# One decode layer on one core: a single ordered stream of cache loads over six 32 KB tiles, with the projections and the ending in column layout

## The chip, the cores and the metric

The kernel runs on one core of a Trainium2 chip. The metric is device time in microseconds (us). Quoted times are medians of the executions in the fast state; the spans in the profiles are about 2 us shorter than the device time. A ratio is the mean time of one kernel's fast runs over the mean of the kernel before's fast runs of the same rounds, so it is not quite the ratio of the medians.

How to read the profile: PE is TensorE's products, PEld its weight loads, DVE is VectorE, ACT ScalarE, POOL GpSimd, SP SyncE; "SPq" is SP's instruction queue. "L147" is line 147 of the kernel that the profile belongs to. A bracket such as `[1.36 <-issue]` gives the idle time of the engine before the instruction and what ended it; "issue" means that the engine waited for nothing that the profile shows.

## The reference, cut to what matters

```python
B, Sq, D, H, Sk, Dh, F = 2, 1, 512, 32, 8192, 128, 1376      # all data bf16
n = layernorm(x)                                            # [B, 1, D]
q = (n @ wq).reshape(B, 1, H, Dh)                           # wq [512, 4096]
p = softmax(q . k_cache * Dh**-0.5)                         # k_cache [B, H, 8192, 128]
o = p @ v_cache                                             # v_cache [B, H, 8192, 128]
h = x + o.reshape(B, 1, H * Dh) @ wo                        # wo [4096, 512]
g = layernorm(h)
out = h + (relu(g @ W_gate) * (g @ W_up)) @ W_down           # F = 1376
```

One token of each of two sequences attends to 8192 cached keys and values, each head with its own cache. K and V are 134 MB each, and every byte is used once. All the weights together are 12.6 MB.

## The kernel before

It takes the 64 heads of both batch entries one after the other. K of a head is a 16 KB row in each of 128 partitions, and VectorE makes the scores of one head: a product with q (the same in all partitions), four halving additions and a reduction. TensorE makes p·V for two heads at a time, with p as the two-column stationary operand and V moving. The parts that the change touches:

```python
# q: 64 products with one output row; the row goes through DRAM to be spread over the partitions
with tc.tile_pool(name="wq", bufs=1) as wq_pool, tc.tile_pool(name="qc", bufs=3) as qcpool:
    wq_sb = wq_pool.tile([P, KC, Hq * Dh], bf16)                 # 32 KB a partition
    nc.sync.dma_start(out=wq_sb, in_=...)
    for b in range(B):
        for n8 in range(NQC):
            # ... 4 matmuls into qps [1, 512], copied to qch [1, 512] ...
            nc.sync.dma_start(out=qdram[b, n8 * 512:(n8 + 1) * 512], in_=qch[0:1, :])
# the wq pool ends here, and the pools below get its space
qrep = qrep_pool.tile([P, B, Hq * Dh], bf16)
nc.sync.dma_start(out=qrep, in_=qdram_b)                         # partition step 0: 2.1 MB
kpool (3 x 16 KB), vgpool (2 x 32 KB), prodpool (2 x 16 KB) = ...

for b in range(B):
    for g in range(NG):                                          # two heads
        for j in range(G):                                       # one head
            nc.sync.dma_start(out=kt, in_=A_k_cache[b, h]...)    # K on SP's queue
            nc.scalar.dma_start(out=vg[:, j], in_=A_v_cache[b, h]...)   # V on ACT's
            nc.vector.tensor_tensor(out=prod, in0=kt, in1=qh, op=ALU.mult)
            # ... halving adds in prod, reduce to scol, exp into pg, the sum of p ...
        for t in range(NT):
            nc.tensor.matmul(out=ops[2, 256], lhsT=pg[:, :, t], rhs=V of both heads at t, ...)

# attention's pools end here; only then is there room for wo
nc.gpsimd.dma_start(out=wo_sb, in_=A_wo.rearrange("(h d) n -> d h n", d=P))
# ... W_gate, W_up, W_down on the SP and ACT queues ...
for b in range(B):
    for h in range(Hq):                                          # rows of 512
        nc.tensor.matmul(out=aps[1, 512], lhsT=ocols[:, b, h:h + 1], rhs=wo_sb[:, h, :], ...)
    # residual and layernorm on one partition
# ... gate and up: weights stationary, 2 columns moving; down: rows of 512 again ...
```

The softmax here doesn't subtract the row's maximum and nothing guards it: scores larger than these inputs give would overflow.

## Time and profile before

| | before |
|---|---|
| median of 4 runs beside the changed kernel (lowest to highest) | 721.05 us (720.52 to 723.4) |
| span in the profile | 719.8 us |
| DMA: bytes, mean rate | 283.56 MB, 394 GB/s |
| VectorE busy | 602.4 us, 84% |
| TensorE products busy, mean granted clock | 346.4 us, 0.744 |

The kernel is bound by its loads. These lines of its profile page show VectorE's busy share in tenths, the DMA engines' busy share in tenths, and the rate, in 40 equal slices of 18.0 us:

```profile
...
DVE  1007999999999999999999989999999999999612
...
DMA  9739699999999999999999999999999999999970
GB/s 371 328 154 429 249 420 383 429 426 428 427 427 425 429 423 427 430 426 427 428 425 428 427 427 427 425 427 427 428 425 429 426 425 428 428 424 432 343 267 1
...
```

VectorE starts late and is then nearly as busy as DMA. From 126 us to 665 us every slice moves about 427 GB/s. At that rate 283.56 MB take 664 us. The rest of the 719.8 us is lost in holes, and they can be added up from the last row: in the first seven slices (371, 328, 154, 429, 249, 420, 383) some 27.6 us, in the last four (432, 343, 267, 1) some 28.0 us, and in between next to nothing. The Trainium skill ("DMA: Bandwidth & Descriptors", Where 436 GB/s comes from) gives the fabric's ceiling as 435 GB/s; 427 is 2% under it.

The largest early hole, in a table of stretches (after the busy times and counts of PE, PEld, DVE, ACT and POOL come PE's granted clock, the DMA engines' busy share and the GB/s):

```profile
...
30.00:40.00 10.00, 10.00 (x43) 3.64 (x42) 0.00 (x0) 5.89 (x11) 0.00 (x0) 1.00 0.20 83
40.00:46.00 6.00, 4.26 (x20) 1.52 (x19) 0.00 (x0) 4.54 (x7) 0.00 (x0) 1.00 0.00 1
46.00:50.00 4.00, 0.00 (x0) 0.00 (x0) 0.00 (x0) 0.23 (x1) 0.00 (x0) 0.89 0.74 262
...
```

From 30 to 46 us, while TensorE makes q, less than 1 MB is loaded. The costliest groups of instructions (after the bar: busy time, mean ns of one; after the second bar: idle time just before them, and what ended most of it):

```profile
...
L170 DVE TENSOR_TENSOR prod<-kt,qrep 128x8192 bf16<-128x8192 bf16 x64 | 283.2, 4425 | 72.9 <-DMA kt<-in_A_k_cache_dram 72.9
...
L250 PE MATMUL aps<-wo_sb,ocols 128*1 128x512 bf16 x64 | 14.0, 379 | 1.1 <-DMA wo_sb<-in_A_wo_dram 1.1
...
L309 PE MATMUL dps<-wd_sb,hmlp_cols 128*1 128x512 bf16 (+1 forms) x22 | 7.8, 540 | 0.5 <-DVE hmlp_cols L296 0.5
...
```

VectorE waits for K for 72.9 us in all. In the ending, 64 wo products of 512 columns take 14.0 us, and the 22 of W_down 7.8 us. The same ending holds the cheap form as well. In the timeline (start, duration, instruction, count), gate and up have weights stationary and only two columns moving, and four products start every 0.11 us, one per 27 ns:

```profile
...
705.38 0.25 PE L278 MATMUL gu_ps<-hncols,wg_sb 128*128 128x2 bf16 x4 [0.26 <-ACT hncols L271]
...
705.49 0.25 PE L285 MATMUL gu_ps<-hncols,wu_sb 128*128 128x2 bf16 x4
...
```

### The profile page before, as it was taken

The page shows a single profiled execution, that of the slowest core. Times are in us where ns is not written, and L with a number is a line of the kernel's source. Part 1 is how long each engine was busy: PE and PEld are TensorE (multiplying, and loading weights), DVE is VectorE, ACT ScalarE, POOL GpSimd, SP SyncE. Part 2 cuts the span into 40 slices and gives each one's busy share as a digit, 9 for nine tenths or more (in the row PEclk, how much of TensorE's full clock was granted, in tenths as well). Part 3 has the DMA queues.
Part 4 walks back from the last instruction along what each step waited for, and adds up shares of the span by engine and source line. Part 5 has one row for each costly group of instructions (what it writes and reads, how often), then busy time and mean ns, then how long its engine had stood idle before and what let it go on. Part 6 is the DMA issues. An engine that isn't in the chain of part 4 may idle for free.

```text
span 719.8 us, 6035 instructions
## 1 busy us (share of the span) xinstructions
PE 346.4 (48%) x2431; PEld 221.6 (31%) x2431; DVE 602.4 (84%) x412; ACT 60.2 (8%) x252; POOL 3.7 (1%) x12
## 2 busy tenths in 40 slices
PE   0440454554443455455544444554555444444896
PEld 0110233332232333333332223333333322333543
DVE  1007999999999999999999989999999999999612
ACT  1140000000000000000000000000000000000010
POOL 1000000000000000000000000000000000000000
PEclk9985577787667776777777776677776777667797
DMA  9739699999999999999999999999999999999970
GB/s 371 328 154 429 249 420 383 429 426 428 427 427 425 429 423 427 430 426 427 428 425 428 427 427 427 425 427 427 428 425 429 426 425 428 428 424 432 343 267 1
DMA packets 22735, 283.56 MB, mean 394 GB/s; under 512 B 2242, under 2 KB 3636, under 8 KB 5684
## 3 DMA queue, kind: packets, MB, share of 16 engines
q1 hardware_dynamic: 11748, 143.25, 47.6%
q10 hardware_dynamic: 9856, 135.73, 44.7%
q0 software_dynamic: 1104, 4.20, 1.7%
q8 instruction: 19, 0.31, 0.2%
q14 instruction: 8, 0.07, 0.0%
HBM read 283.15 MB, written 0.02 MB: 393 GB/s over the span
## 4 chain that ended last, share of the span: by engine, by line
DMA 47%; DVE 40%; issue 7%; PE 6%; ACT 0%; SPq 0%; DVEq 0%; POOLq 0%; ACTq 0%
DMA kt<-in_A_k_cache_dram 41%; DVE prod L170 21%; DVE prod L174 18%; DMA wq_sb<-in_A_wq_dram 4%; DMA wo_sb<-in_A_wo_dram 2%; PE qps L121 2%; PE aps L250 2%; PE dps L309 1%; DVE scol L182 1%; PE gu_ps L278 0%; PE gu_ps L285 0%; DMA qdram<-qch 0%; DVE stats L78 0%; DVE h_rows L256 0%; DVE outr L316 0%
## 5 line engine op out<-in xcount | busy, mean ns | idle before, releaser
L201 PE MATMUL ops<-vg,pg 128*2 128x256 bf16 x2048 | 294.1, 316 | 252.8 <-DMA vg<-in_A_v_cache_dram 220.5
L170 DVE TENSOR_TENSOR prod<-kt,qrep 128x8192 bf16<-128x8192 bf16 x64 | 283.2, 4425 | 72.9 <-DMA kt<-in_A_k_cache_dram 72.9
L201 PEld LDWEIGHTS <-pg 128*2 128x2 bf16 x2048 | 196.6, 97 | 392.0 <-issue 232.1
L174 DVE TENSOR_TENSOR prod<-prod 128x4096 bf16<-128x4096 bf16 (+3 forms) x256 | 281.7, 1155 | 0.0
L186 ACT ACTIVATE pg<-scol 128x64 bf16<-128x64 f32 x64 | 16.4, 256 | 366.9 <-DVE scol L182 366.5
L192 PE MATMUL zrow_ps<-zcb,ones_col 128*1 128x1 bf16 x64 | 11.2, 175 | 74.5 <-ACT zcb L191 71.2
L182 DVE TENSOR_REDUCE scol<-prod 128x64 f32<-128x512 bf16 x64 | 43.8, 684 | 0.1
L206 ACT ACTIVATE orows<-ops 2x256 bf16<-2x256 f32 x32 | 11.7, 366 | 226.6 <-PE ops L201 226.6
L121 PE MATMUL qps<-wq_sb,xncols 128*1 128x512 bf16 x64 | 15.9, 412 | 15.0 <-DMA wq_sb<-in_A_wq_dram 15.0
L209 PEld LDWEIGHTS <-orows 2*128 2x128 bf16 x64 | 3.5, 93 | 45.0 <-ACT orows L206 45.0
L250 PE MATMUL aps<-wo_sb,ocols 128*1 128x512 bf16 x64 | 14.0, 379 | 1.1 <-DMA wo_sb<-in_A_wo_dram 1.1
L121 PEld LDWEIGHTS <-xncols 128*1 128x1 bf16 x64 | 5.6, 88 | 24.9 <-issue 18.3
L191 ACT ACTIVATE zcb<-zcols 128x1 bf16<-128x1 f32 x64 | 12.7, 204 | 2.0
L186 ACT ACTIVATION_READ_ACCUMULATOR pg<-scol 128x1 f32 x64 | 11.9, 187 | 0.1
L256 DVE TENSOR_TENSOR h_rows<-aps,x_rows 1x512 f32<-1x512 f32 x2 | 1.4, 680 | 12.1 <-PE aps L250 12.1
L209 PE MATMUL ocols_ps<-ident,orows 2*128 2x1 bf16 x64 | 6.4, 166 | 10.6 <-ACT orows L206 9.4
L128 ACT ACTIVATE qch<-qps 1x512 bf16<-1x512 f32 x16 | 9.4, 586 | 22.1 <-PE qps L121 22.1
L250 PEld LDWEIGHTS <-ocols 128*1 128x1 bf16 x64 | 5.4, 84 | 9.3 <-issue 0.7
L309 PE MATMUL dps<-wd_sb,hmlp_cols 128*1 128x512 bf16 (+1 forms) x22 | 7.8, 540 | 0.5 <-DVE hmlp_cols L296 0.5
L78 DVE BATCH_NORM_STATS2 stats<-x_rows 1x6 f32<-1x512 f32 x2 | 1.4, 678 | 7.8 <-DMA x_rows<-in_A_x_dram 7.8
L316 DVE TENSOR_TENSOR outr<-dps,h_rows 1x512 f32<-1x512 f32 x2 | 1.4, 679 | 6.4 <-PE dps L309 6.4
L102 PE MATMUL xncols_ps<-ident,xn_rows 1*128 1x1 bf16 x8 | 0.5, 166 | 12.8 <-DVE xn_rows L85 12.8
(42 smaller groups left out, 36.1 us busy)
## 6 DMA issues: line engine op xcount, KB each, us to landing
vg<-in_A_v_cache_dram ACTq DMA_DIRECT2D x64, 2048.0 KB
kt<-in_A_k_cache_dram SPq DMA_DIRECT2D x64, 2048.0 KB
wq_sb<-in_A_wq_dram SPq DMA_DIRECT2D x1, 4096.0 KB
wo_sb<-in_A_wo_dram POOLq DMA_DIRECT2D x1, 4096.0 KB, 17.8
qrep<-qdram SPq DMA_DIRECT2D x1, 2048.0 KB
wg_sb<-in_B_W_gate_dram SPq DMA_DIRECT2D x1, 1376.0 KB
wu_sb<-in_B_W_up_dram ACTq DMA_DIRECT2D x1, 1376.0 KB
wd_sb<-in_B_W_down_dram SPq DMA_DIRECT2D x1, 1280.0 KB
```

The costliest lines, as they stand in the source:

```text
L121: nc.tensor.matmul(out=qps[0:1, :], lhsT=xncols[:, c, b:b + 1], rhs=wq_sb[:, c, n8 * 512:(n8 + 1) * 512], start=(c == 0), stop=(c == KC - 1),)
L170: nc.vector.tensor_tensor(out=prod, in0=kt, in1=qh, op=ALU.mult)
L174: nc.vector.tensor_tensor(out=_view(prod, 0, [[Dh, NT], [1, half]]), in0=_view(prod, 0, [[Dh, NT], [1, half]]), in1=_view(prod, half, [[Dh ...
L182: nc.vector.tensor_reduce(out=scol, in_=_view(prod, 0, [[Dh, NT], [1, 8]]), axis=AXIS.X, op=ALU.add,)
L186: nc.scalar.activation(out=pg[:, j, :], in_=scol, func=ACT.Exp, accum_out=zcols[:, b, h:h + 1], scale=SCALE,)
L191: nc.scalar.activation(out=zcb, in_=zcols[:, b, h:h + 1], func=ACT.Copy)
L192: nc.tensor.matmul(out=zrow_ps[0:1, b, h:h + 1], lhsT=ones_col[:, :], rhs=zcb[:, :], start=True, stop=True,)
L201: nc.tensor.matmul(out=ops[:, :], lhsT=pg[:, :, t], rhs=rhs, start=(t == 0), stop=(t == NT - 1),)
L206: nc.scalar.activation(out=orows, in_=ops, func=ACT.Copy)
L209: nc.tensor.matmul(out=ocols_ps[:, b, h:h + 1], lhsT=orows[0:G, j * Dh:(j + 1) * Dh], rhs=ident[0:G, j:j + 1], start=True, stop=True,)
L250: nc.tensor.matmul(out=aps[0:1, :], lhsT=ocols[:, b, h:h + 1], rhs=wo_sb[:, h, :], start=(h == 0), stop=(h == Hq - 1),)
L309: nc.tensor.matmul(out=dps[0:1, :], lhsT=hmlp_cols[0:w, c, b:b + 1], rhs=wd_sb[0:w, c, :], start=(c == 0), stop=(c == FC - 1),)
```

## The change

The intent is to let nothing interrupt the load stream. Its core, cut from a long diff (the kernel is mostly rewritten):

```diff
+ring = tc.tile_pool(name="ring", bufs=6)            # six tiles of 32 KB a partition, for everything large
+wq_sb = ring.tile([P, KC, Hq * Dh], bf16, tag="s")  # wq is the first of them: K need not wait for its space
-qps [1, 512] -> qch -> qdram -> qrep                # q through DRAM
+xnb = x normalised, each value copied to 64 columns # so that the product itself spreads q over partitions
+for half in range(2):                               # even head: partitions 0..63, odd head: 64..127
+    for c in range(KC):
+        nc.tensor.matmul(out=qps[half * 64:(half + 1) * 64], lhsT=xnb[:, b, c, :],
+                         rhs=wq_v[:, c, g * QP:(g + 1) * QP, half, :], ...)
+def load_pair(eng, cache, b, i):                    # two adjacent heads are one run: 128 rows of 32 KB
+    t = ring.tile([P, T2, Dh], bf16, tag="s", name="kv")
+    eng.dma_start(out=t, in_=cache[b, 2*i:2*i+2].rearrange("h s d -> (h s) d").rearrange("(p t) d -> p t d", p=P))
+load_k, load_v: both on nc.sync                     # one FIFO: K0 V0 K1 V1 ...
-prod = prodpool.tile(...)                           # the scores are made in the K tile itself,
+nc.vector.tensor_tensor(out=kt, in0=kt, in1=qb, op=ALU.mult)   # a pair per instruction
-nc.tensor.matmul(out=ops, lhsT=pg[:, :, t], rhs=V at t, 256 columns)
+nc.tensor.matmul(out=o[:, j, :], lhsT=vt[:, t, :], rhs=pm[:, t, :])   # V stationary, 2 columns moving
 ...
+# the last loads: K(N-2) K(N-1) V(N-2) wo V(N-1) W_gate W_up W_down, all in the ring
+pm_a = scores(N-2); weighted_v(N-2); zi = inverse_z(1)
+pm_b = scores(N-1)
+ocols[1] = o_ps[1] * zi
+project_o(0); project_o(1)                          # wo for 31 of the 32 pairs, after the last score
+weighted_v(N-1); project_o(2)                       # the last pair
+layernorm in columns: sums over partitions by products with a matrix of 1/D
+wo and W_down: weights stationary, every fourth column of a 512-column row (128 columns, step 4)
+out stored from columns
```

## The prediction

> **What bounds it now.** The load stream. In the table of stretches DMA moves 427 GB/s at a DMA share of 1.0 from 200 to 660 us; VectorE is about 95% busy there and waits only for K (72.9 us in the list of waits). The Trainium skill ("DMA: Bandwidth & Descriptors", Where 436 GB/s comes from) puts the fabric ceiling at 435 GB/s; the trace agrees within 2%. 283.6 MB at 427 GB/s is 664 us; the span is 719.8, so 56 us are holes: about 2.5 us at the start, 15.6 us at 30 to 50 us (q goes through DRAM: 83, 1, 262 GB/s), 9 us at 65 to 120 us (tiles come free late, as VectorE started at 58.6 us), and 28 us after 670 us (wo waits for the attention pools; then 14.0 us of wo matmuls, the MLP, 7.9 us of down projection, with few loads).
>
> **What changes.**
> - The q round trip and its 2.1 MB go; 281.05 MB remain.
> - One FIFO with six 32 KB slots. VectorE starts when the first K pair lands (about 22 us). K(n+3) waits for the scores of n, done about 30 us before its turn (estimate): no hole.
> - VectorE per pair: the same elements in half as many instructions. The trace shows 18.4 us for two heads when nothing waits; I expect 18.0 to 18.5 us, 580 to 592 in all. DMA needs 19.65 us per pair, so VectorE waits for K.
> - PE: 4096 loads of 128 columns with N=2 matmuls. The gate/up lines of before have this form: 80 in 2.1 us, 26 ns each at granted clock 0.5; one pair's V takes about 3.5 us. This fits the skill ("TensorE: Matmul & The Clock Gate", Fast Weight Load): full 128-column bf16 weights load fast[...].
> - wo and w_down keep 1 KB rows. In 680 to 686 us these move about 346 GB/s, so 5.6 MB cost 16.2 us, not 13.1.
>
> **Sum.** Start 2.5 us; 275.4 MB at 427 GB/s = 645 us; 1 KB rows 16 us: loads end at E = about 663 us. Tail: the last K lands about E-42; VectorE (the last two pairs are interleaved) ends its scores about E-15. Then PE, in order: V of pair N-2 (3.5 us), 248 wo loads (6.5 us at 26 ns, if a stride of four elements loads as fast), last V (3.5), layernorm (3), gate/up (2.5), down (1.2), small steps and the store (3 to 4). That ends about E+9: span about 672, device time about 1.5 more: **673.5 us**. Gain 48: about 16 from the q gap, 9 from the refill, 19 from the ending, 5 from 2.1 MB less, minus 1.
>
> **Range.** 667 to 685 us, 8 times in 10. Faster by over 2%: 0.97; within 2%: 0.02; slower: 0.01.
>
> **What would show the steps right.** 425 to 429 GB/s in all slices but the first and the last two; VectorE's first product at about 22 us, and 580 to 592 us busy; the chain of waits nearly all DMA of K/V tiles until the last 20 us; V matmuls 26 to 60 ns apart; under 12 us between the last load's landing and the end.
>
> **What would make it wrong.** (a) One queue with 32 KB rows doesn't hold 427 GB/s, or has a gap at each of its 72 loads: 0.3 us each is 20 us. (b) Strided wo/w_down weights don't load fast: at 60 to 100 ns, 300 loads add 10 to 22 us. (c) Slots come free later than I think, since SP waits in order for both VectorE and PE. (d) Larger contiguous rows move over 430 GB/s: each 1% is 6.5 us.

## The result, and the profile after

| | before | after |
|---|---|---|
| median of 4 runs (lowest to highest) | 721.05 us (720.52 to 723.4) | 684.17 us (683.88 to 684.38) |
| ratio (95% interval) | | 0.948 (0.947 to 0.950) |
| span | 719.8 us | 682.2 us |
| DMA | 283.56 MB, mean 394 GB/s | 281.67 MB, mean 413 GB/s |
| VectorE busy | 602.4 us | 596.6 us |
| TensorE products busy, granted clock | 346.4 us, 0.744 | 139.5 us, 0.529 |

It is 5.2% faster, and inside the predicted range, though 10.7 us above the predicted 673.5. The result agrees with the reference; so does that of every experiment below, the two with deliberately wrong weights included, as noted there. The same rows of the page after (slices of 17.1 us):

```profile
...
DVE  0499999999998999999799999999999899999901
...
DMA  9999999999999999999999999999999999999980
GB/s 369 430 432 433 433 433 431 431 429 426 431 429 434 428 429 431 427 427 427 431 430 432 429 431 429 427 431 428 431 429 434 431 427 431 432 429 401 362 318 2
...
```

The holes of the first 126 us are gone, and the plateau is a little higher (426 to 434). What is left is a first slice of 369 and an end of 401, 362, 318 and 2. The groups:

```profile
...
L147 DVE TENSOR_TENSOR kv<-kv,qrep 128x16384 bf16<-128x16384 bf16 x32 | 278.0, 8689 | 18.1 <-DMA kv<-in_A_k_cache_dram 15.4
...
L176 PEld LDWEIGHTS <-kv 128*128 128x128 bf16 x4096 | 114.0, 104 | 507.4 <-issue 345.4
...
L245 PEld LDWEIGHTS <-wo_sb 128*128 128x128 bf16 x256 | 9.1, 119 | 3.9 <-issue 3.9
...
```

VectorE now waits for K for 15.4 us instead of 72.9. TensorE loads V 4096 times, in full 128 columns, and wo 256 times. VectorE's start (the conversion of x, then the first product):

```profile
...
22.79 0.17 DVE L111 CAST xc<-xc_bf 128x8 f32<-128x8 bf16 x1 [21.57 <-DMA xc_bf<-in_A_x_dram]
...
28.87 8.69 DVE L147 TENSOR_TENSOR kv<-kv,qrep 128x16384 bf16<-128x16384 bf16 x1 [2.67 <-ACT qrep L138]
...
```

W_down, the last load, is issued at 647.2 us and takes 17.2 us, so it lands at 664.4 us:

```profile
...
L235 SPq DMA_DIRECT2D wd_sb<-in_B_W_down_dram x1: 618/618/618, 647.2 to 647.2; - x1
...
DMA to landing us min/median/max: 17.2/17.3/17.3
```

From there to the end are 17.8 us. The stretches before that landing (columns as above) show that its last 4 us run at half the DMA share:

```profile
...
655.00:660.00 5.00, 3.56 (x107) 3.47 (x105) 0.00 (x0) 0.00 (x0) 0.00 (x0) 0.50 0.99 371
660.00:664.00 4.00, 3.40 (x102) 3.40 (x103) 0.00 (x0) 0.00 (x0) 0.00 (x0) 0.50 0.53 166
...
```

And the timeline of the end, which matters most below:

```profile
...
647.47 1.22 DVE L159 TENSOR_REDUCE sc<-kv 128x128 f32<-128x1024 bf16 x1
...
652.00 0.77 PE L245 MATMUL a_ps<-oc_208,wo_sb 128*128 128x1 bf16 x19
...
654.13 3.79 PE L245 MATMUL a_ps<-oc_208,wo_sb 128*128 128x1 bf16 x109 [1.36 <-issue]
657.78 0.77 PE L245 MATMUL a_ps<-oc_209,wo_sb 128*128 128x1 bf16 x19
...
660.60 3.52 PE L245 MATMUL a_ps<-oc_209,wo_sb 128*128 128x1 bf16 x101 [2.05 <-issue]
...
663.99 0.86 PE L176 MATMUL ops_207<-pm_92,kv 128*128 128x2 bf16 x27
...
666.25 2.85 PE L176 MATMUL ops_207<-pm_92,kv 128*128 128x2 bf16 x101 [1.40 <-issue]
...
672.91 2.91 PE L276 MATMUL gu_ps<-ln2n,wgu 128*128 128x2 bf16 x88 [0.75 <-DVE ln2n L106]
...
676.31 1.60 PE L292 MATMUL y_ps<-act,wd_sb 128*128 128x2 bf16 x44 [0.49 <-DVE act L284]
...
678.14 0.41 SPq L299 DMA_DIRECT2D out_dram<-y  x1
```

The last reduction of VectorE ends at 648.7 us. TensorE then does the wo products of 31 pairs (652.0 to 664.0), V of the last pair (to 669.1), and the MLP (to 677.9), and the store goes out at 678.1. When the last byte lands, TensorE is still busy with work whose data came long before.

### Where the 37.6 us of span came from

A sum over the GB/s rows separates three parts. Ideal time is bytes over plateau rate: 283.56 MB at 427 GB/s are 664 us, and 281.67 MB at 430 GB/s are 655 us.

| part | before | after | gained | predicted |
|---|---|---|---|---|
| bytes over plateau rate | 664 | 655 | 9 | 4 (5 for 2.1 MB less, and minus 1) |
| lost in the first 126 us | 27.6 | 2.4 | 25 | 25 (16 + 9) |
| lost in the last slices | 28.0 | 25.3 | 3 | 19 |
| sum | 719.7 | 682.7 | 37 | 48 |

The sum is exact to about half a microsecond only. The front half of the prediction was right in size, the stream was slightly better than thought, and the ending was worth 3 us instead of 19.

### The profile page after: what moved, and what is told of

It is laid out like the page before. It is cut to its first block, busy times and chain, and to the rows that moved or that the text cites. A ratio compares the mean times of both kernels' runs of the same rounds, so it can differ in the third digit from the quotient of the medians.

```text
span 682.2 us, 9754 instructions
## 1 busy us (share of the span) xinstructions
PE 139.5 (20%) x4562; PEld 135.0 (20%) x4562; DVE 596.6 (87%) x220; ACT 35.6 (5%) x145; POOL 1.7 (0%) x10
## 2 busy tenths in 40 slices
DMA packets 16183, 281.67 MB, mean 413 GB/s; under 512 B 1712, under 2 KB 7184, under 8 KB 7184
## 4 chain that ended last, share of the span: by engine, by line
DMA 50%; DVE 42%; PE 5%; issue 2%; ACT 1%; DVEq 0%; ACTq 0%
DMA kv<-in_A_k_cache_dram 47%; DVE kv L151 19%; DVE kv L147 19%; DMA xc_bf<-in_A_x_dram 3%; DVE sc L159 3%; PE a_ps L245 1%; PE ops_206 L176 1%; PE ops_207 L176 1%; PE ops_205 L176 1%; PE gu_ps L276 0%; PE qps L132 0%; ACT pm_92 L164 0%; PE y_ps L292 0%; PE zb L182 0%; ACT pm_90 L164 0%
## 5 line engine op out<-in xcount | busy, mean ns | idle before, releaser
L147 DVE TENSOR_TENSOR kv<-kv,qrep 128x16384 bf16<-128x16384 bf16 x32 | 278.0, 8689 | 18.1 <-DMA kv<-in_A_k_cache_dram 15.4
L151 DVE TENSOR_TENSOR kv<-kv 128x2048 bf16<-128x2048 bf16 (+3 forms) x128 | 275.8, 2158 | 4.1
L176 PEld LDWEIGHTS <-kv 128*128 128x128 bf16 x4096 | 114.0, 104 | 507.4 <-issue 345.4
L159 DVE TENSOR_REDUCE sc<-kv 128x128 f32<-128x1024 bf16 x32 | 39.0, 1220 | 3.0
L176 PE MATMUL ops_206<-pm_90,kv 128*128 128x2 bf16 x512 | 14.2, 165 | 80.1 <-ACT pm_90 L164 80.1
L176 PE MATMUL ops_206<-pm_86,kv 128*128 128x2 bf16 x512 | 14.2, 165 | 67.2 <-ACT pm_86 L164 67.2
L176 PE MATMUL ops_205<-pm_90,kv 128*128 128x2 bf16 x512 | 14.2, 165 | 63.7 <-ACT pm_90 L164 63.7
L176 PE MATMUL ops_205<-pm_92,kv 128*128 128x2 bf16 x512 | 14.2, 165 | 62.8 <-ACT pm_92 L164 62.8
L176 PE MATMUL ops_206<-pm_88,kv 128*128 128x2 bf16 x512 | 14.2, 165 | 62.5 <-ACT pm_88 L164 62.5
L176 PE MATMUL ops_205<-pm_86,kv 128*128 128x2 bf16 x512 | 14.2, 165 | 61.9 <-ACT pm_86 L164 61.9
L176 PE MATMUL ops_205<-pm_88,kv 128*128 128x2 bf16 x512 | 14.2, 165 | 60.7 <-ACT pm_88 L164 60.7
L176 PE MATMUL ops_206<-pm_92,kv 128*128 128x2 bf16 x384 | 10.7, 165 | 46.9 <-ACT pm_92 L164 46.9
L164 ACT ACTIVATE pm_90<-sc 64x128 bf16<-64x128 f32 x16 | 5.5, 346 | 165.8 <-DVE sc L159 165.6
L164 ACT ACTIVATE pm_88<-sc 64x128 bf16<-64x128 f32 x16 | 5.5, 346 | 145.2 <-DVE sc L159 145.0
L164 ACT ACTIVATE pm_86<-sc 64x128 bf16<-64x128 f32 x16 | 5.5, 346 | 133.9 <-DVE sc L159 133.7
L164 ACT ACTIVATE pm_92<-sc 64x128 bf16<-64x128 f32 x16 | 5.5, 346 | 130.1 <-DVE sc L159 129.9
L245 PEld LDWEIGHTS <-wo_sb 128*128 128x128 bf16 x256 | 9.1, 119 | 3.9 <-issue 3.9
L132 PE MATMUL qps<-wq_sb,xnb 128*64 128x512 bf16 x64 | 8.7, 435 | 1.2 <-DVE xnb L114 1.2
L132 PEld LDWEIGHTS <-xnb 128*64 128x64 bf16 x64 | 4.6, 122 | 4.8 <-issue 1.7
## 6 DMA issues: line engine op xcount, KB each, us to landing
wgu<-in_B_W_gate_dram SPq DMA_DIRECT2D x1, 1376.0 KB, 17.2
```

What stands on the lines that cost most here:

```text
L132: nc.tensor.matmul(out=qps[half * HALF:(half + 1) * HALF], lhsT=xnb[:, b, c, :], rhs=wq_v[:, c, g * QP:(g + 1) * QP, half, :], start=(c == ...
L147: nc.vector.tensor_tensor(out=kt, in0=kt, in1=qb, op=ALU.mult)
L151: nc.vector.tensor_tensor(out=_view(kt, 0, [[Dh, T2], [1, half]]), in0=_view(kt, 0, [[Dh, T2], [1, half]]), in1=_view(kt, half, [[Dh, T2], ...
L159: nc.vector.tensor_reduce(out=sc, in_=_view(kt, 0, [[Dh, T2], [1, 8]]), axis=AXIS.X, op=ALU.add)
L164: nc.scalar.activation(out=pm[ps, :, half], in_=sc[ps, :], func=ACT.Exp, accum_out=zm[ps, b, i, half:half + 1], scale=SCALE)
L176: nc.tensor.matmul(out=o[:, j, :], lhsT=vt[:, t, :], rhs=pm[:, t, :], start=(t == 0), stop=(t == T2 - 1))
```

## The experiments

Twelve kernels ran, in three groups of four, each group on one chip beside its own runs of the kernel before (medians 721.2, 720.0 and 720.95 us). One run of the kernel before, at 748.41 us, was slow and is left out. The kernel after did not run in these groups. Differences to after (684.2 us) are therefore between groups, and the kernel before moves by up to 1.2 us from group to group.

| kernel | built on | median us (range) | ratio (95%) |
|---|---|---|---|
| q_proj | before | 713.61 (713.07 to 714.22) | 0.990 (0.988 to 0.991) |
| q_proj_space | before | 724.10 (723.40 to 724.77) | 1.004 (1.002 to 1.006) |
| q_proj_space2 | before | 701.57 (701.13 to 701.85) | 0.974 (0.972 to 0.976) |
| two_queues | after | 694.74 (692.21 to 695.57) | 0.964 (0.962 to 0.965) |
| two_queues_inorder | after | 683.23 (682.93 to 683.46) | 0.949 (0.946 to 0.951) |
| wo_early | after | 678.72 (678.64 to 678.97) | 0.941 (0.939 to 0.943) |
| wo_early2 | after | 673.32 (673.23 to 673.43) | 0.935 (0.933 to 0.937) |
| x_first | after | 684.64 (684.52 to 684.73) | 0.951 (0.948 to 0.953) |
| v_moving | after | 690.62 (690.31 to 691.65) | 0.958 (0.957 to 0.960) |
| row_ending | after | 691.27 (690.77 to 691.77) | 0.959 (0.957 to 0.960) |
| wo_rows | after | 682.50 (682.19 to 683.05) | 0.947 (0.945 to 0.948) |
| wo_early2_rows | wo_early2 | 671.53 (671.33 to 671.82) | 0.931 (0.930 to 0.933) |

### 1. q_proj: the broadcast projection alone, in the kernel before

Question: is the 16 us hole the trip of q through DRAM, as the prediction said, or the space of wq, which the K tiles reuse?

```diff
+xnb = misc.tile([P, KC, B, P], bf16)
+nc.vector.tensor_copy(xnb, xncols.unsqueeze(3).to_broadcast([P, KC, B, P]))
-qps = psum2.tile([1, 512], ...);  lhsT=xncols[:, c, b:b + 1]
+qps = psum2.tile([P, 512], ...);  lhsT=xnb[:, c, b, :]
-nc.scalar.activation(out=qch, in_=qps[0:1, :], func=ACT.Copy)
-nc.sync.dma_start(out=qdram[b, n8 * 512:(n8 + 1) * 512], in_=qch[0:1, :])
+nc.scalar.activation(out=qrep[:, b, n8 * 512:(n8 + 1) * 512], in_=qps, func=ACT.Copy)
-nc.sync.dma_start(out=qrep, in_=qdram_b)
```

> The kernel before, with q broadcast to all partitions by the projection itself, no trip through DRAM; everything else as it was. My prediction put the 15.6 us hole at 30 to 50 us down to that trip. Theory A (the hole is the wq tile's space: K tiles lie where wq lies, so no K load starts before the last projection matmul at about 44 us): K still starts at about 44 us, only the 2.1 MB of the trip (about 5 us) and 2 us of start go: 712 to 716 us. Rival B (the trip is the hole): the hole closes and VectorE starts by about 35 us: 697 to 700 us.

It gained 7.5 us, to 713.6. The hole stayed. In the waits of SP's queue (total, times, longest), the issue of K waits for the last q product, although nothing goes through DRAM any more:

```profile
...
SPq L151 <- PE qps L122: 15.8, 1, 15.8
...
```

L151 is the load of K. K's tiles lie where wq was, so they can't be issued before TensorE has read all of wq; VectorE's first product moved only from 58.6 to 51.9 us. The trip was worth the 7.5 us, of which 2.1 MB at 427 GB/s are 5. The space of wq is left as the hole's cause; run 3 puts it to the test.

### 2. q_proj_space: and wq in space of its own — confounded by one buffer

```diff
+wq_ctx = ctx.enter_context(ExitStack())             # the wq pool stays open through attention
-prodpool = attn_ctx.enter_context(tc.tile_pool(name="prodpool", bufs=2))
+prodpool = attn_ctx.enter_context(tc.tile_pool(name="prodpool", bufs=1))   # to make room
```

> As q_proj, but wq has SBUF of its own until the end (the product tile has one buffer instead of two to make room; VectorE works in order, so that should cost nothing). K loads can start at once behind wq. Theory A: the hole at 30 to 50 us closes, VectorE starts at 30 to 36 us: 694 to 700 us, so the rest of the way to 684 is the ending. Rival B: no further gain over q_proj.

The hole closed (VectorE started at 38.2 us, and DMA moved over 420 GB/s between 30 and 50 us), and yet the kernel took 724.1 us, a little slower than before. My statement that one product buffer costs nothing was wrong. VectorE's timeline in mid-stream:

```profile
...
299.18 4.42 DVE L165 TENSOR_TENSOR prod<-kt,qrep 128x8192 bf16<-128x8192 bf16 x1
...
309.19 4.42 DVE L165 TENSOR_TENSOR prod<-kt,qrep 128x8192 bf16<-128x8192 bf16 x1
...
```

The heads follow each other at 10.0 us, above the 9.8 us that DMA needs for one (4.19 MB at 427 GB/s). VectorE had become the bound. In the kernel before, with two product buffers, the scheduler mixes the additions of one head with those of the next; here each of a head's six instructions needs the one before it. Same elements, same instructions, and each takes as long by itself (the first addition 2292 ns here, 2287 ns in before). What differs is how they follow each other: from 200 to 600 us the median instruction of before starts 84 ns before the end of the one in front, and here 34 ns after it. That is 118 ns per instruction. (The busy time, 635.3 us instead of 602.4, shows only the lost overlap, 33 us / 384 = 86 ns, and not the new gap.) The Trainium skill ("VectorE: DVE Perf Modes", The DRAIN you can't avoid) says that chained operations cost the same with a semaphore after each as without; these two traces show that an instruction which needs the result just before it costs more than one that doesn't. With pairs, the changed kernel has half as many such steps.

### 3. q_proj_space2: the same with both product buffers

Room was found by reusing two rows of x for h, so that no buffer of the stream had to go.

```diff
 wq_ctx = ctx.enter_context(ExitStack())             # as above, and not closed before the ending
 prodpool = attn_ctx.enter_context(tc.tile_pool(name="prodpool", bufs=2))
-h_rows = misc.tile([1, B * D], f32)
-hn_rows = misc.tile([1, B * D], bf16)
+h_rows = x_rows
+hn_rows = xn_rows
```

> q_proj_space again without its flaw: there the single product buffer kept VectorE from interleaving two heads, and a head cost 10.0 us instead of 9.2, so VectorE became the limit. Here both product buffers stay (room comes from reusing the x and xn rows for h and hn). Theory A (the hole at 30 to 50 us was K tiles waiting for wq's space): VectorE starts at about 38 us as in q_proj_space, a head costs 9.2 us, time 697 to 705 us. Rival (the start doesn't matter, the stream refills anyway): 710 us or more, as q_proj (713.6).

701.6 us, as expected, 12.0 us under q_proj (10.8 when each is counted from the kernel before of its own group). The stretches (columns as before) show the hole closed and another one later, where the tiles of K and V come free late:

```profile
...
30.00:40.00 10.00, 10.00 (x36) 4.00 (x35) 1.64 (x1) 4.78 (x8) 0.00 (x0) 1.00 1.02 433
...
55.00:60.00 5.00, 2.38 (x14) 1.43 (x15) 5.00 (x6) 0.94 (x6) 0.00 (x0) 0.50 0.32 134
...
```

So the hole of 16 us is the space of wq. In the changed kernel wq is only one of six tiles, and the hole is not there either (430 to 433 GB/s in the slices of that time).

### 4. and 5. two_queues and two_queues_inorder: is one FIFO worth anything in itself?

```diff
 def load_v(n):
-    vts[n] = load_pair(nc.sync, A_v_cache, *seq[n])
+    vts[n] = load_pair(nc.scalar, A_v_cache, *seq[n])
```

> The kernel after with the V loads issued from ACT's queue, K and weights from SP's. Theory: one queue isn't worth anything by itself, the same 16 engines are full either way (DMA share 1.0 in both kernels): within 1% of after, though the first K pair lands later (wq and K share with V) and VectorE starts at about 40 us instead of 28.9 and catches up at about 1 us per pair. Rival (the order of arrival of one FIFO matters): VectorE is late to the end, or holes show, and it is 1 to 3% slower, 691 to 705 us.

two_queues took 694.7 us, 10.6 more than after, which looked like proof that one FIFO matters. The trace said otherwise. With another queue the scheduler also ordered VectorE differently: it mixed the chains of two pairs, and VectorE then stood waiting for the next K in the middle of a chain.

```profile
...
87.48 8.69 DVE L147 TENSOR_TENSOR kv<-kv,qrep 128x16384 bf16<-128x16384 bf16 x1 [9.18 <-DMA kv<-in_A_k_cache_dram]
...
```

Such waits for K came to 58.7 us, against 15.4. The rate shows what they cost: three slices in mid-stream fall to 392, 341 and 371 GB/s, and from 200 to 400 us it is 419 GB/s instead of 430 (waits for K alone would prove nothing: the kernel before had 72.9 us of them in a full stream). two_queues_inorder repeats the edit with the product of each pair pinned behind the reduction of the pair before:

```diff
-nc.vector.tensor_tensor(out=kt, in0=kt, in1=qb, op=ALU.mult)
+with (tc.issue_after(last[0]) if last else nullcontext()):
+    nc.vector.tensor_tensor(out=kt, in0=kt, in1=qb, op=ALU.mult)
```

> two_queues again (V from ACT's queue) with VectorE's order of instructions pinned to that of after: in two_queues the scheduler had interleaved pairs two by two, so that a product waited for the next pair's K in the middle of a chain and two slots came free at once. Theory (that order was the loss, two queues cost nothing): 682 to 688 us. Rival (the arrival order of two queues is the loss): 691 to 697 us as two_queues (694.7).

683.2 us, as after (684.2). The GB/s rows of the two pages, two_queues first, and what VectorE waited for in two_queues_inorder (total, times, longest):

```profile
...
GB/s 370 448 427 425 423 435 415 426 392 434 421 341 432 405 430 410 418 433 371 434 402 428 425 426 426 430 434 428 417 434 428 427 429 424 425 428 426 362 403 26
...
GB/s 371 431 435 432 430 430 430 430 428 435 430 428 434 430 432 430 432 429 428 430 430 430 430 430 433 430 430 428 430 430 430 430 431 428 430 430 413 351 334 3
...
DVE zi L189 <- PE zb L185: 28.1, 3, 18.9
...
```

In the stream two queues cost nothing (430 GB/s in both); a changed order on VectorE does. The equal time in all is partly chance, because the ending changed as well. The normalisation of the 15 pairs before the last now stood on VectorE between the last pair's product and its additions, and waited 18.9 us for TensorE, which itself stood waiting for wo. So the scores ended at 663.7 us, 15 us later than in after; but half of the wo products ran at 643.8 us already. Only the streams of these two runs can be compared with after, and not their ends. The Trainium skill ("DMA: Bandwidth & Descriptors", Issuing engines are not separate DMA queues) says that transfers from several engines share the same 16 DMA engines, and that a second issuer saves only issue time; the stream of this run agrees.

### 6. wo_early: wo before V of the last-but-one pair, and its products before the last score

This tests the theory that the missing gain lies in the order of work on TensorE after the last score. The rival was that the last load sets the end anyway.

```diff
-split = [(0, 0, NP), (1, 0, NP - 1), (1, NP - 1, NP)]
+split = [(0, 0, NP), (1, 0, NP - 3), (1, NP - 3, NP)]    # the last group holds three pairs
 load_k(N - 2); load_k(N - 1)
-load_v(N - 2); load wo
+load wo; load_v(N - 2)
+inverse_z(1) and ocols[1] = ... moved to the scores of pair N-3
+project_o(0); project_o(1)                                # before the last two scores
 pm_a = scores(N-2); weighted_v(N-2); pm_b = scores(N-1)
-project_o(0); project_o(1)
```

> The kernel after with wo loaded one place earlier (before V of the last pair but one), the wo products of 29 of 32 pairs put before the last two pairs' V on TensorE, and the last group of three pairs instead of one. Theory (the ending of after is set by TensorE's serial work after VectorE's last score: 33.5 us from 648.7 to 682.2 us, of which the wo products with their refill gaps are 12.1): the wo products run while VectorE still works, and the end is set by the last load's landing at about 664 plus 44 w_down products and the store, 6 us: span 669 to 672, time 670 to 674 us. Rival (the landing of the last loads plus a fixed tail sets it already): no more than 3 us gained, 681 to 685 us.

678.7 us: faster than after, but a miss of 670 to 674. The group's normalisation stood on VectorE in front of the last pairs, and it needs the V products of an earlier pair:

```profile
...
593.08 3.55 PE L176 MATMUL ops<-pm,kv 128*128 128x2 bf16 x128 [15.89 <-ACT pm L164]
...
597.13 0.32 DVE L186 RECIPROCAL zi<-zb 128x26 f32<-128x26 f32 x1 [5.03 <-PE zb L182]
...
```

VectorE waited 5.0 us for TensorE there, the last two pairs were mixed as well, and it ended its scores at 652.7 us instead of 648.7.

### 7. wo_early2: the same with VectorE's order pinned, and the normalisation one pair later

```diff
+split = [(0, 0, NP), (1, 0, NP - 2), (1, NP - 2, NP)]
 pm_a = scores(N-2)
+with tc.issue_after(last[0]):                              # after the last-but-one score
+    zi = inverse_z(1); ocols[1] = o_ps[1] * zi
+project_o(0); project_o(1)                                # while VectorE makes the last score
+weighted_v(N-2)
 pm_b = scores(N-1)                                        # every product pinned as in two_queues_inorder
 weighted_v(N-1); project_o(2)
```

> wo_early again, with VectorE's order pinned: pairs one after the other, and the small normalisation of the early group behind the last score but one. In wo_early that normalisation stood on VectorE in front of the last pairs and waited 4 us for TensorE, and the last two pairs were interleaved, so VectorE ended at 652.7 us, 4 us later than in after. Theory: VectorE ends at 648 to 650 us, the rest of TensorE's work is short, and the end is set by the last load (about 665 us) plus w_down's products and the store, 6 us: span 670 to 672, time 670 to 674 us. Rival: another fixed tail holds, 677 to 680 us as in wo_early (678.7).

673.3 us, as expected: 10.9 us under after (and 11.3 under x_first, which ran beside it and equals after), 6.5% under the kernel before, and so faster than both. Its end:

```profile
...
633.89 5.12 PE L248 MATMUL a_ps<-oc,wo_sb 128*128 128x1 bf16 x149 [17.36 <-DMA wo_sb<-in_A_wo_dram]
...
640.56 3.17 PE L248 MATMUL a_ps<-oc,wo_sb 128*128 128x1 bf16 x91 [1.54 <-issue]
...
649.02 1.22 DVE L162 TENSOR_REDUCE sc<-kv 128x128 f32<-128x1024 bf16 x1
...
654.99 1.01 PE L179 MATMUL ops<-pm,kv 128*128 128x2 bf16 x32 [0.54 <-DMA kv<-in_A_v_cache_dram]
...
665.58 1.62 PE L296 MATMUL y_ps<-act,wd_sb 128*128 128x2 bf16 x44 [2.04 <-DMA wd_sb<-in_B_W_down_dram]
...
667.44 0.41 SPq L303 DMA_DIRECT2D out_dram<-y  x1
```

The wo products run as soon as wo lands (633.9 us), under VectorE's last pair, and now the last load ends the kernel: the 44 products of W_down wait 2.0 us for it, and from its landing to the end are under 6 us. The same number of products, of the same form, as in after; what differs is their place in TensorE's order, the place of one load, two pairs instead of one in the last group, and the pinned order of VectorE. No run of after has the pin alone. But VectorE's last score ends at 650.2 us here, 1.5 us later than in after, so the 10.9 us don't come from a faster VectorE. This is the main finding.

### 8. x_first: the late start of VectorE

```diff
-nc.scalar.dma_start(out=xc_bf, in_=A_x.rearrange("b s (p c) -> p (b s) c", p=P))
+nc.sync.dma_start(out=xc_bf, in_=A_x.rearrange("b s (p c) -> p (b s) c", p=P))   # ahead of wq, same queue
```

> The kernel after with the 2 KB of x issued first on the same queue as all loads (in after it lay on ACT's queue in 8-byte pieces and landed at 22.8 us, behind the bulk loads). VectorE's first product starts at 21 to 23 us instead of 28.9. Theory (VectorE has 0.9 us of slack per pair and works the late start off by about 100 us; the loads set the pace): 682 to 685 us, no gain. Rival (the start's 7 us carry through): 676 to 679 us.

x landed at 2.6 instead of 22.8 us, and the first product came 5.3 us earlier:

```profile
...
23.60 8.69 DVE L147 TENSOR_TENSOR kv<-kv,qrep 128x16384 bf16<-128x16384 bf16 x1 [17.59 <-DMA kv<-in_A_k_cache_dram]
...
```

The time did not change (684.6 us). VectorE needs 18.6 us per pair and DMA 19.5 (8.39 MB at 430 GB/s), so 5 us of lateness can be made up within six pairs.

### 9. v_moving: p stationary and V moving, as before

```diff
-nc.tensor.matmul(out=o[:, j, :], lhsT=vt[:, t, :], rhs=pm[:, t, :], ...)
+nc.tensor.matmul(out=orow[2, 128], lhsT=pm[:, t, :], rhs=vt[:, t, :], ...)
+# then a copy to bf16 and one transposing product for each pair
```

> The kernel after with the products with V the other way round, as in before: the probabilities (2 columns) stationary, V moving (128 columns per product), then a transposing product for each pair. Theory: in the stream TensorE has 19.5 us per pair and needs 3.6 now, 7 to 14 then, so nothing shows in the stream; only the last pair or two, after VectorE's last score, get longer: 4 to 10 us each, 690 to 705 us. Rival (V stationary is worth nothing even there): 682 to 686 us.

690.6 us, 6.4 more than after. TensorE's products are busy 196 of the 400 us from 200 to 600 us instead of 75, and DMA still moves 430 GB/s there: in the stream the stationary side doesn't matter. It counts in the end, twice:

```profile
...
647.68 10.14 PE L177 MATMUL orow<-kv,pm 128*2 128x128 bf16 x128 [25.56 <-ACT pm L164]
...
659.19 7.63 PE L249 MATMUL a_ps<-oc,wo_sb 128*128 128x1 bf16 x224
...
666.75 9.19 PE L177 MATMUL orow<-kv,pm 128*2 128x128 bf16 x128
...
```

V of a pair takes 9.2 to 10.1 us instead of 3.55. The cost is not the full 12 us because the wo products between them ran without the gaps that after has (see the last experiments).

### 10. row_ending: wo, layernorm and W_down in rows, as before

```diff
-for c in range(KC): nc.tensor.matmul(out=a_ps[:, b, c:c + 1], lhsT=wo_v[:, h, :, c], rhs=ocols[k] column h)
+nc.tensor.matmul(out=aps[b][1, 512], lhsT=ocols[k] column h, rhs=wo_sb[:, h, :])
+# layernorm of each row on one partition, transposed by eight products; W_down in rows of 512
-NM = 4;  spool bufs=3
+NM = 2;  spool bufs=2                                     # to make room
```

> The kernel after with the ending of before: outputs of wo and w_down in one row (one column of activations stationary, 512 columns of weights moving), layernorm in rows on one partition, x and the result in rows. Theory (the column layout pays): 64 wo products of 512 columns take 14 us at full clock to 27 us at half, against 12.1; layernorm 2 us more; 22 w_down products 5 to 8 us more; 1 us more for the row adds: 692 to 709 us. Rival (column loads with their refill gaps are no better): 682 to 688 us.

691.3 us, 7.1 more than after, just under the expected range, which allowed for a clock at half during the wo products; it was 0.85.

```profile
...
651.65 15.95 PE L252 MATMUL aps<-wo_sb,oc 128*1 128x512 bf16 x62
...
679.90 6.86 PE L311 MATMUL dps<-wd_sb,act 128*1 128x512 bf16 x22 [0.49 <-DVE act L304]
...
```

62 wo products of 512 columns take 15.95 us at a granted clock of 0.85 where 248 of one column take 12.0 at 0.50; W_down takes 6.86 instead of 1.60 us. The column form is right, and it is not where the expected gain was lost.

### 11. and 12. wo_rows and wo_early2_rows: the 1 KB rows of wo (the weights are deliberately wrong)

Loading wo as one 32 KB run for each partition puts its rows in the wrong places. Same bytes, same instructions. The comparison with the reference did not notice, presumably because its tolerance is wider than this error. So it says little about wo in the other runs either; neither kernel is usable.

```diff
-nc.sync.dma_start(out=wo_sb, in_=A_wo.rearrange("(h d) n -> d h n", d=P))
+nc.sync.dma_start(out=wo_sb, in_=A_wo.rearrange("(d h) n -> d h n", d=P))
```

> The kernel after with wo read so that each partition gets one run of 32 KB instead of 32 rows of 1 KB: the result is wrong on purpose, the bytes are the same. Theory (the ending of after waits for VectorE and TensorE, not for loads): the last loads land 2 to 3 us earlier and the time stays, 683 to 685 us. Rival (1 KB rows are on the path): 680 to 682 us.

> The same wrong wo in wo_early2, where the last load sets the end. Theory: here the 1 KB rows are on the path, 2 to 3 us faster than wo_early2: 670 to 671.5 us. Rival (1 KB rows move as fast as others, the dip in the last slices has another cause): 673 to 673.5 us.

In wo_early2_rows wo landed at 631.7 instead of 633.9 us, and the end came 1.8 us earlier (671.5 against 673.3). 4.19 MB take 9.75 us at 430 GB/s, and 2.2 us more make 351 GB/s (an estimate, worked out from these numbers). With the length of the rows the order of the addresses changed too; the two were not separated. Where the last load ends the kernel, nearly all of it counts.

wo_rows came out between the two expectations (682.5 us against 683 to 685 and 680 to 682), and so decides nothing by its time. VectorE's end and the wo products didn't move. But the gap of 1.40 us in front of the 101 last V products of after is gone; here they run in one piece:

```profile
...
663.78 3.55 PE L176 MATMUL ops<-pm,kv 128*128 128x2 bf16 x128
...
```

The gaps are worth a look. In after they stand at 654.13, 660.60 and 666.25 us, 1.36, 2.05 and 1.40 us long, with nothing to wait for ("issue"), and between two of them lie 109 + 19 and 101 + 27 products, 128 each time: with their weight loads 256 instructions. The Trainium skill ("Runtime: NRT & Kernel Launch", Instruction fetch mechanics) says that instruction memory is refilled by DMA in blocks of 256 instructions, and that the cost of crossing a block is "mostly hidden". The spacing agrees; the cost is not hidden here, where TensorE takes two instructions every 27 to 34 ns for microseconds on end. The trace holds these fetches, on a queue of their own (packets, MB, share of the 16 engines):

```profile
...
q8 instruction: 35, 0.57, 0.3%
...
```

Each is 16 KB. In after three of them land at 652.85, 659.23 and 664.87 us, and TensorE goes on 1.3 to 1.4 us after each. Between two of these landings it started 256 instructions and then stood still. The same holds for all 16 such gaps ("issue", over 0.8 us, after 635 us) in eight of the traces: the last fetch landed 1.2 to 1.5 us before TensorE went on. So in the gaps TensorE waits for its next instructions. In the stream each pair's V is 256 instructions and then a pause of some 16 us; the fetch falls into the pause, and no gap shows. The bulk loads did not slow the transfers themselves: in after a fetch takes 1.0 to 1.2 us in the stream and 1.0 to 1.3 us in the ending. What differs is when it starts. In wo_rows the third starts at 661.44 us instead of 663.77, and the third gap is gone; in v_moving none comes too late for the 224 wo products. What sets that start was not found.

## Why the prediction was right or wrong

The verdict (faster by over 2%) and the range were right; the point was 10.7 us too low.

**Right: what bounds it, and the stream.** All slices but the first and the last few move 426 to 434 GB/s. VectorE waits for K for 15.4 us in all, and the loads ended at 664.4 us where 663 was predicted. The plateau is 430 rather than 427 GB/s, which is about 4.6 us over 281.67 MB; the thin last slices took it back. So E came out right partly by luck: two errors of some 4 us cancelled. The slow 1 KB rows were foreseen (346 GB/s; the trace has this from 680 to 684 us, and 307 over the 680 to 686 us that the prediction names), and the estimate from wo_early2_rows, 351 GB/s, agrees.

**Right: the cost of TensorE's new form.** The V weights load every 27 ns (127 in 3.46 us), as read from gate and up before the change. With a step of four elements, wo's 128 loads in 4.35 us are 34 ns (start to start 33, as for W_down's 43, which move two columns as V does). The 96-column loads of gate and up start 80 ns apart, before and after. So the strided form is close to the packed one, which fits the Trainium skill ("TensorE: Matmul & The Clock Gate", Weight-path perf modes), where fast loading is allowed packed or strided; but 26 ns was not to be had.

**Right in size, wrong in cause: the hole of 15.6 us.** The prediction put it down to "q goes through DRAM". q_proj took the trip away and the hole stayed; q_proj_space2 gave wq its own space and it closed. The two together gained 18.4 us over the kernel before of the same group. That the predicted gain of 16 us came all the same was luck: the change gave wq a tile of the ring as well as taking the trip away.

**Wrong without effect: VectorE's start.** 28.9 us instead of 22, because x, sent in 272 tiny packets by another queue, landed at 22.8 us behind wq. x_first moved it and the time stayed. Its 596.6 us busy are also over the predicted 580 to 592.

**Wrong: "Tail: ... That ends about E+9".** This is the step that failed: the tail was to take 9 us from the last landing, and under 12 was named as the sign; it took 17.8. The end of the scores was predicted at E-15, 648 us, and came at 648.7. From there the prediction's list sums to about 24 us; the trace has 33.5:

| step after the last score | predicted us | measured us |
|---|---|---|
| V of pair N-2; measured: exponentials, table load and sum, which hide it | 3.5 | 3.3 |
| wo of 31 pairs | 6.5 | 12.0 |
| last V | 3.5 | 5.1 |
| layernorm | 3 | 2.9 |
| gate and up | 2.5 | 2.95 |
| down | 1.2 | 1.65 |
| small steps and the store | 3 to 4 | 5.6 |

So the path was the one foreseen, and the terms were mis-sized. wo is 248 x 34 ns = 8.4 us and two waits for instructions (3.4 us), which the prediction did not have; the last V holds the third. The small steps are the last pair's normalisation, wo products and residual add (0.85), the activation (0.45), the add (0.2) and the store (4.05).

**The larger omission: order.** The order does not explain the miss of the number, since the prediction's own list had it. But it wrote this list down as a sequence after the last score and did not ask why wo had to be in it. Only 2 of the 64 heads need the last scores. wo_early2 moves the rest under VectorE's last pair and gets 10.9 us, more than the gaps (4.8) and the slower loads (2) together, and most of the 16 us by which the ending fell short of the expected 19. With the old forms of the products the changed kernel is 7.1 us (row_ending) and 6.4 us (v_moving) slower, and still its ending as a whole gained only about 3 us over before. wo_early2 says why in part: in after these products stand in line after the last score.

The steps from before to the best kernel, in medians: 721.0, without the trip 713.6, wq in its own space 701.6, the rest of the change 684.2, wo's products early 673.3 (from four groups of runs, whose kernels before lie within 1.2 us).

**Open.** (a) From 660 to 664 us the loads run at 166 GB/s and a DMA share of 0.53 as if about half of the engines had finished; which and why was not followed. (b) What sets the start of an instruction fetch, and so the length of the gaps. (c) How much of the 17 to 18 us between q_proj_space2 and after comes from the later refill hole and how much from the ending was not separated.

## What to carry to other kernels

In a kernel bound by one stream, look first at what the first tiles of the stream wait for: space that an earlier tile still holds can stop it for longer than the visible trip through memory. For the ending, list what truly depends on the last score, and put everything else in front of it in the engine's order, with its data loaded that much earlier; then the last load ends the kernel. Before believing a comparison of queues or buffers, compare the order of instructions on each engine, since a small edit can change it and cost more than the thing under test; and compare the endings too, since two equal times can hide two different ones.

## What the Trainium skill lacked or had wrong

- "DMA: Bandwidth & Descriptors", Where 436 GB/s comes from, says that for HBM to SBUF the HBM side, about 358 GB/s, binds. With one core running, this case moved 430 GB/s from HBM over 400 us, near the 435 that the same section gives for the fabric. (The page's section Bandwidth adds that its 425 GB/s is a single-core number; that is the one that applies.)
- "DMA: Bandwidth & Descriptors", Specifications, gives 512 B as the smallest transfer at line rate. wo in rows of 1 KB took 2.2 us longer than in rows of 32 KB, about 351 against 430 GB/s (an estimate; the order of the addresses differed too).
- "Runtime: NRT & Kernel Launch", Instruction fetch mechanics, calls the cost of crossing 256 instructions mostly hidden. On TensorE, at 27 to 34 ns for a load and a product, it showed as gaps of 1.36, 2.05 and 1.40 us, each ending 1.3 to 1.4 us after a fetch of 16 KB landed.
- "VectorE: DVE Perf Modes", The DRAIN you can't avoid, has no cost for depending on the instruction just before. The same instructions started 34 ns after the end of the one in front (median) as dependent chains, and 84 ns before it when two heads were mixed: 118 ns for each.
- "TensorE: Matmul & The Clock Gate", Weight-path perf modes, allows a column step in fast weight loads but gives no cost for it: 27 ns packed, 33 to 34 ns with a step of four elements, at granted clock 0.5.
